# One core: a chunk's sums are split one chunk later, and ScalarE copies products before it splits operands

## The chip, the cores and the metric

The kernel runs on one core of a Trainium2 chip. The metric is the device time of one execution in microseconds. The core has TensorE (PE, matrix products), VectorE (DVE), ScalarE (ACT), GpSimd (POOL) and SyncE (SP, which here only issues DMAs). Each engine works through its own instructions in the order in which they were written; an instruction that waits holds up everything behind it on that engine.

## The reference

The program computes, for 4 batches of 448 rows:

```
attn = sigmoid(q k^T / sqrt(64) - log(448)) v           # 12 heads of 64
h    = relu(x w_in);  u, v = halves of h (512 each)     # x: 768 wide
v_n  = (v - mean) / sqrt(var + 1e-6)
x    = (u * (w_spatial v_n + b_spatial)) w_out          # back to 768
xn   = (x - mean) / sqrt(var + 1e-6) * g_ln
out  = x + relu(xn w_ch1) w_ch2                         # 768 -> 3072 -> 768
```

Everything is float32. Each operand of a product is split into a rounded high part and a remainder, and each product is three matmuls (high x high, high x low, low x high).

## The kernel before, in words

Attention and the first block (hv, hu, spatial) come first and fill some 330 us. Then come the stages that the change touches.

**Projection (class Project, the loop over NCH = 14 chunks of 128 rows).** A chunk is a row block of x. `step(c)` does, on each engine in this order:

- TensorE: 24 matmuls of chunk c, then the six transposes of chunk c - 2 (`turn`, L679).
- ScalarE: copies chunk c out of PSUM (L634); scales the transposes of chunk c - 2 by g_ln (six L681, into a stage); casts their halves to high parts (L299, an instruction for two operands and one for a third); casts the sums of chunk c - 2 (L299).
- VectorE: normalises chunk c - 1 (L649); statistics of chunk c (two L489, one L491); subtracts high parts from the halves (two L300) and from the sums (one L300) of chunk c - 2, which gives the remainders; prepares the scale of chunk c (L482, `rs`).
- GpSimd: four subtractions on the stage of chunk c - 2 (L686 to L689), which give the sums in the one buffer `t`; then the power that makes the scale of chunk c out of `rs` (L483).
- SP: stores the chunk (L635), and from chunk 7 on also the split operands (L670, `out`), since the second half's operands wait in memory.

The halves and sums are the operands of a seven-product scheme (two by two blocks with seven instead of eight products): R11, R21, T2 come from the halves, T1, T3, R22 and T4 from the sums. For chunks 0 to 6 the fourth sum goes into a buffer of its own (`t4`), and `last_sums` splits it for all seven chunks at once. Chunks 7 to 13 put four sums into `t`. A stage has two buffers, `t` has one, the stored operands have one buffer for the first three and two for the sums.

During chunks 9 to 12 the loop also makes the first group's weight sums (`left.sums`, four GpSimd instructions L753 to L756), and splits three of them (`left.put`).

**Groups (function mlp).** Each of 24 rounds (two halves of the rows, 12 groups of 256 hidden units) multiplies in the order L11 R11, L12 R21, S2 T2, S1 T1, S3 T3, L22 T4, S4 R22. L and S are weight operands, R and T row operands. The products share a few PSUM buffers: `pa` takes L11 R11, S2 T2, S3 T3 and L22 T4 one on top of the other, and ScalarE copies it between (`ta`, `tb`, `tc_`, L866, L883, L891); TensorE may add the next product to `pa` only when the copy is done. VectorE adds `pb` and `pd` to those copies; `put` makes the hidden units with a relu (L853) and their remainder (L854).

Round k = 0 also has what the projection left over: the turns of chunks 12 and 13, the normalisation of chunk 13, the splits of the remaining weights, and the next round's weight sums on VectorE. At its end SP loads the two weights of the second half of the round (`w2c`, `w2d`, L726) and the rows for the final sum; `w2c.split` and `w2d.split` (L735 on ScalarE, L736 on GpSimd) stand before the next round's first copy.

Of the kernel before, what the change touches and what calls it, by code (L numbers as in the profile page):

```python
# [18 lines left out]
B, H, S, D = 4, 12, 448, 64  # L19
# [20 lines left out]
HCH = HT // P  # L40
KH = KC // 2
# [182 lines left out]
def sigmoid_attention_gmlp_mlp(ctx: ExitStack, tc, q, k, v, w_in, w_sp, w_out, g_ln, w1, w2, out):  # L224
# [73 lines left out]
    def split(hi, lo, x, eng=nc.vector):  # L298
        nc.scalar.copy(hi, x)  # L299
        eng.tensor_sub(lo, x, hi)  # L300
# [311 lines left out]
    class Project:  # L612
# [4 lines left out]
        def __init__(self, wo, gb, ys_r, xn_r, stage_r, t, t4):  # L617
            self.wo, self.gb, self.ys_r, self.xn_r, self.stage_r = wo, gb, ys_r, xn_r, stage_r
            self.t, self.t4 = t, t4
            self.late, self.turns, self.out_r, self.out_t = None, [], None, None  # L620

        def step(self, c, g):
# [14 lines left out]
            mv = norm_stats([y2[:, 0], y2[:, 1]])  # L637
            if len(self.turns) > 1:
                self.turn()
# [32 lines left out]
        def turn(self):  # L672
# [17 lines left out]
            if c >= HCH:  # L690
                self.out_now = self.out_t.next()
            split(*self.parts(c, 0, 2), x1)
            split(*(a[:, 0] for a in self.parts(c, 2, 1)), x2[:, 1])
            self.out(c, 0, 3)
            n = 3 if c < HCH else 4
            split(*self.parts(c, 3, n), t[:, :n])
# [72 lines left out]
    def mlp(first, proj, after):  # L769
# [58 lines left out]
        for k, (h, g) in enumerate(todo):  # L828
# [33 lines left out]
            pa = ps1()  # L862
            if k == 0:
                left.put("S1", "S3")
            P_(pa, "L11", "R11", True)
            nc.scalar.copy(ta, pa[:, :S])  # L866
# [3 lines left out]
            if k == 0:  # L870
                left.put("L22")
                proj.norm()
# [4 lines left out]
            if k == 0:  # L877
                left.put("S4")
                proj.turn()
                nxt.sums(nc.vector)  # L880
            pre.pop(1)
            P_(pa, "S2", "T2", False)
            nc.scalar.copy(tb, pa[:, :S])  # L883
            pd = ps1()
            P_(pd, "S1", "T1", True)
            pre.pop(2)
# [6 lines left out]
            if k == 0:  # L893
                proj.turn()
                nxt.put("L11", "L12")
            next(chunks, None)
            put(1, 1, tc_)
            if k:
                w2c.load()
                if nxt:  # L900
                    nxt.put("L11")
# [9 lines left out]
            if k == 0:  # L911
                nxt.put("S1", "S3")
# [227 lines left out]
    for c in range(NCH):  # L1140
# [6 lines left out]
        elif c == HCH:  # L1147
            left.load()
        elif c == HCH + 1:
            proj.last_sums()  # L1150
        elif c == HCH + 2:
            left.sums()
            after.load()
        elif c > HCH + 2 and c < HCH + 6:
            left.put(("L11", "L12", "S2")[c - HCH - 3])
# [76 lines left out]
```

## Time and profile before

Three runs took 1114.56, 1116.41 and 1117.33 us, median 1116.41. The profiled execution took 1114.5 us, with a span of 1112.7 us.

| stretch, us | what runs | us | TensorE busy, us | granted clock |
|---|---|---|---|---|
| 331.0 to 360.4 | chunks 3 to 8 | 29.40 | 29.40 | 1.00 |
| 360.4 to 380.6 | chunks 9 to 12 | 20.20 | 19.84 | 1.00 |
| 380.6 to 396.5 | chunk 13, first two products | 15.90 | 11.44 | 0.79 |
| 396.5 to 418.8 | rest of round 0 | 22.30 | 15.22 | 0.77 |
| 418.8 to 427.1 | round 1, first two products | 8.30 | 5.70 | 0.79 |
| 427.1 to 430.4 | round 1, third product | 3.30 | 3.27 | 0.51 |
| 430.4 to 445.0 | round 1, rest | 14.60 | 14.01 | 1.00 |

Times are microseconds from the span's start. Chunks and products are named by what TensorE works on, and it runs ahead of the other engines by one or two chunks. A clock of 1.00 is 2.4 GHz, 0.50 is 1.2 GHz; values between are means over a stretch. A wait is put down to the instruction that released it last. Over the whole span TensorE is busy 96%, VectorE 62%, ScalarE 41%, GpSimd 29%.

### The profile page before, as it was taken

What the parts mean: (1) busy time and instruction counts of PE and PEld (TensorE: products, weight loads), DVE (VectorE), ACT (ScalarE), POOL (GpSimd) and SP (SyncE); (2) the same over time, 40 slices, a digit from 0 to 9 for tenths busy, and PEclk for the clock granted to TensorE, in tenths of its full rate; (3) what the DMA queues carried; (4) which work ended last, traced back from release to release, by engine and by line L of the source; (5) the groups of instructions that cost most, each with busy time, mean ns of one, the idle gap of its engine ahead of it and who ended that gap; (6) DMA issues with size and microseconds to landing.
All of it is one profiled execution on the core that took longest, in us unless ns stands there. A gap on an engine that the chain in (4) does not pass through costs nothing.

```text
span 1112.7 us, 15188 instructions
## 1 busy us (share of the span) xinstructions
PE 1064.4 (96%) x5644; PEld 926.0 (83%) x5644; DVE 690.8 (62%) x1072; ACT 459.4 (41%) x820; POOL 321.3 (29%) x292
## 2 busy tenths in 40 slices
PE   8999999999999878999999999899999999999997
PEld 5466666668899867888888888899999999999997
DVE  4743446447657766888888898853555555555543
ACT  6755556554537654333333333320422222222210
POOL 1231212202207643333222233343322222222210
PEclk9999999999999888999999999999999999999999
DMA  8756869835522557555455455478411111111103
GB/s 239 221 170 203 277 173 337 302 120 183 162 76 101 202 209 269 164 185 164 156 178 183 153 169 171 151 314 275 126 57 57 58 57 57 58 57 57 58 29 100
DMA packets 72730, 174.54 MB, mean 157 GB/s; under 512 B 12560, under 2 KB 31376, under 8 KB 71632
## 3 DMA queue, kind: packets, MB, share of 16 engines
q1 hardware_dynamic: 68368, 151.73, 42.1%
q0 software_dynamic: 3168, 19.73, 5.0%
q10 hardware_dynamic: 1120, 2.11, 0.6%
q8 instruction: 44, 0.72, 0.3%
q14 instruction: 30, 0.25, 0.1%
HBM read 126.67 MB, written 46.87 MB: 156 GB/s over the span
## 4 chain that ended last, share of the span: by engine, by line
PE 67%; DVE 16%; issue 7%; ACT 4%; POOL 3%; DMA 2%; SPq 0%; POOLq 0%; DVEq 0%; ACTq 0%
PE ps L269 19%; PE ps L270 18%; PE ps L271 18%; PE ps L466 6%; PE ps L450 5%; DVE f_mlp L290 3%; DVE r_base L300 2%; DVE r_base L854 2%; DVE f_mlp L289 2%; DVE r_mlp L300 2%; DVE f_base L793 2%; DVE f_mlp L293 2%; ACT r_base L853 1%; ACT f_mlp L681 1%; DVE f_mlp L793 1%
## 5 line engine op out<-in xcount | busy, mean ns | idle before, releaser
L269 PE MATMUL ps<-r_mlp,r_base 128*128 128x384 f32 (+1 forms) x946 | 331.6, 351 | 21.0 <-DVE f_base L793 14.8
L270 PE MATMUL ps<-r_mlp,r_base 128*128 128x384 f32 (+1 forms) x946 | 326.4, 345 | 2.9 <-POOL r_mlp L736 2.9
L271 PE MATMUL ps<-r_mlp,r_base 128*128 128x384 f32 (+1 forms) x946 | 325.9, 345 | 0.0
L736 POOL TENSOR_TENSOR r_mlp<-f_base,r_mlp 128x768 fp32r<-128x768 f32 x48 | 91.8, 1914 | 424.4 <-ACT r_mlp L735 424.4
L269 PEld LDWEIGHTS ps<-r_mlp,r_base 128*128 128x128 f32 x946 | 178.4, 189 | 37.8 <-DVE f_base L793 21.2
L270 PEld LDWEIGHTS ps<-r_mlp,r_base 128*128 128x128 f32 x946 | 178.5, 189 | 7.0 <-POOL r_mlp L736 3.4
L271 PEld LDWEIGHTS ps<-r_mlp,r_base 128*128 128x128 f32 x946 | 178.4, 189 | 2.9
L269 PE MATMUL ps<-r_base 128*128 128x448 f32 (+1 forms) x348 | 132.4, 381 | 1.4 <-ACT r_base L299 1.4
L271 PE MATMUL ps<-r_base 128*128 128x448 f32 (+1 forms) x348 | 130.0, 374 | 0.4 <-DVE r_base L300 0.4
L270 PE MATMUL ps<-r_base 128*128 128x448 f32 (+1 forms) x348 | 130.0, 373 | 0.0
L793 DVE TENSOR_TENSOR f_mlp<-ps,f_mlp 128x768 f32<-128x768 f32 (+1 forms) x97 | 91.7, 945 | 51.5 <-PE ps L271 51.4
L454 ACT ACTIVATE f_att<-ps,bias_s 128x896 f32<-128x896 f32 x96 | 91.5, 1005 | 27.4 <-PE ps L450 27.0
L866 ACT COPY f_base<-ps 128x448 f32<-128x448 f32 x24 | 12.8, 533 | 193.4 <-PE ps L271 193.4
L853 ACT ACTIVATE r_base<-f_base 128x448 fp32r<-128x448 f32 x72 | 41.7, 579 | 107.0 <-DVE f_base L909 46.9
L793 DVE TENSOR_TENSOR f_base<-ps,f_base 128x768 f32<-128x768 f32 x72 | 68.6, 953 | 25.0 <-PE ps L271 24.2
L450 PEld LDWEIGHTS ps<-r_att 64*128 64x128 f32 x576 | 51.0, 189 | 36.6 <-issue 20.4
L450 PE MATMUL ps<-r_att 64*128 64x448 f32 x576 | 75.0, 390 | 5.9 <-ACT f_att L454 4.3
L437 POOL TENSOR_TENSOR r_att<-f_att,r_att 128x512 fp32r<-128x512 f32 x22 | 29.9, 1359 | 174.6 <-DVE r_att L433 160.7
L269 PEld LDWEIGHTS ps<-r_base 128*128 128x128 f32 x348 | 65.5, 188 | 15.6 <-issue 6.5
L466 PE MATMUL ps<-f_att 128*64 128x448 f32 x384 | 77.5, 545 | 0.0
L271 PEld LDWEIGHTS ps<-r_base 128*128 128x128 f32 x348 | 65.6, 189 | 8.7 <-DVE r_base L300 0.8
L270 PEld LDWEIGHTS ps<-r_base 128*128 128x128 f32 x348 | 65.7, 189 | 6.6
(131 smaller groups left out, 1568.0 us busy)
## 6 DMA issues: line engine op xcount, KB each, us to landing
f_base<-wscr SPq DMA_DIRECT2D x95, 384.0 KB, 3.7
f_mlp<-in_w SPq DMA_DIRECT2D x56, 384.0 KB, 3.3
f_att<-in_w SPq DMA_DIRECT2D x20, 768.0 KB, 5.4
wscr<-f_mlp SPq DMA_DIRECT2D x56, 192.0 KB, 1.9
wscr<-f_att SPq DMA_DIRECT2D x20, 384.0 KB, 5.9
f_att<-in_v SPq DMA_DIRECT2D x24, 256.0 KB, 5.0
f_base<-in_w_in SPq DMA_DIRECT2D x8, 768.0 KB, 4.7
f_att<-in_k SPq DMA_DIRECT2D x45, 128.0 KB, 5.2
```

The lines of the kernel that those rows point to most:

```text
L269: nc.tensor.matmul(ps, lh, rh, start=first, stop=False, **more)
L270: nc.tensor.matmul(ps, lh, rl, start=False, stop=False, **more)
L271: nc.tensor.matmul(ps, ll, rh, start=False, stop=last, **more)
L290: nc.vector.scalar_tensor_tensor(bits, low, 29, bits, op0=ALU.logical_shift_right, op1=ALU.bitwise_or)
L300: eng.tensor_sub(lo, x, hi)
L437: eng.tensor_sub(kl, kr, kh)
L450: nc.tensor.matmul(ps[:, j, :S], a[w][rows, kc], a[x][rows], start=(i == 0), stop=(i == 2))
L454: nc.scalar.activation(af, ps[:, :, :S], AF.Sigmoid, bias=bias_s, scale=1.0 / math.sqrt(D))
L466: nc.tensor.matmul(a["ps"][rows, :S], a["v"][:, 4 * j + c], af[:, j], start=(c == 0), stop=(c == 3))
L736: nc.gpsimd.tensor_sub(self.lo, self.blk.ap(WC), self.hi)
L793: nc.vector.tensor_add(y[:, hs], ps, y[:, hs])
L853: nc.scalar.activation(hi, src, AF.Relu)
```

## The change

The sums of a chunk are cast and subtracted in a function of their own, `put_sums`, which `step` calls in the following chunk, after that chunk's statistics and before its own turn. `last_sums` moves from chunk 8 to chunk 9. In round 0 ScalarE's copies of the first two products come before the splits of weights that stood ahead of them, the turns of chunks 12 and 13 come later, and three calls of `put_sums` finish chunks 11 to 13. All other rounds are as before.

```diff
@@ class Project
             self.late, self.turns, self.out_r, self.out_t = None, [], None, None
+            self.summed = None
@@ step
             mv = norm_stats([y2[:, 0], y2[:, 1]])
+            self.put_sums()
             if len(self.turns) > 1:
                 self.turn()
@@ turn
             nc.gpsimd.tensor_sub(t4, x1[:, 1], t[:, 1])
-            if c >= HCH:
-                self.out_now = self.out_t.next()
             split(*self.parts(c, 0, 2), x1)
             split(*(a[:, 0] for a in self.parts(c, 2, 1)), x2[:, 1])
             self.out(c, 0, 3)
+            self.summed = c
+
+        def put_sums(self):
+
+            if self.summed is None:
+                return
+            c, self.summed = self.summed, None
             n = 3 if c < HCH else 4
-            split(*self.parts(c, 3, n), t[:, :n])
+            if c >= HCH:
+                self.out_now = self.out_t.next()
+            split(*self.parts(c, 3, n), self.t.ap(4, KH, D)[:, :n])
             self.out(c, 3, n)
@@ mlp
             pa = ps1()
+            P_(pa, "L11", "R11", True)
+            nc.scalar.copy(ta, pa[:, :S])
             if k == 0:
                 left.put("S1", "S3")
-            P_(pa, "L11", "R11", True)
-            nc.scalar.copy(ta, pa[:, :S])
             if late is not None:
                 late.split()
                 late = None
             if k == 0:
-                left.put("L22")
+                proj.put_sums()
                 proj.norm()
             pb = ps1()
             P_(pb, "L12", "R21", True)
             nc.vector.tensor_add(ta, pb[:, :S], ta)
             put(0, 0, ta)
             if k == 0:
-                left.put("S4")
-                proj.turn()
-                nxt.sums(nc.vector)
+                left.put("L22")
             pre.pop(1)
             P_(pa, "S2", "T2", False)
             nc.scalar.copy(tb, pa[:, :S])
+            if k == 0:
+                left.put("S4")
+                nxt.sums(nc.vector)
             pd = ps1()
             P_(pd, "S1", "T1", True)
+            if k == 0:
+                proj.turn()
             pre.pop(2)
...
             nc.vector.tensor_add(tc_, pd[:, :S], tc_)
             if k == 0:
-                proj.turn()
                 nxt.put("L11", "L12")
             next(chunks, None)
             put(1, 1, tc_)
+            if k == 0:
+                proj.put_sums()
+                proj.turn()
...
             put(0, 1, tb)
             if k == 0:
+                proj.put_sums()
                 nxt.put("S1", "S3")
@@ loop over chunks
-        elif c == HCH + 1:
+        elif c == HCH + 2:
             proj.last_sums()
-        elif c == HCH + 2:
             left.sums()
             after.load()
```

Lines after the first insertion are numbered higher in the changed kernel: L649 is L651 there, L686 to L689 are L688 to L691, L735 is L744, L853 and L854 are L862 and L863, L866 is L873.

VectorE, from one normalisation to the next in the middle of the first half (`r_base` 2x192 and 192 are the halves' remainders, `r_mlp` 3x192 the sums'). Before:

```order
L649 TENSOR_SCALAR f_mlp<-f_base,mv,rs 128x768
L489 BN_STATS st_2800<-f_base 128x6 x2
L491 BN_AGGR mv<-st_2800 128x2
L300 TENSOR_TENSOR r_base<-f_mlp,r_base 128x2x192
L300 TENSOR_TENSOR r_base<-f_mlp,r_base 128x192
L300 TENSOR_TENSOR r_mlp<-f_mlp,r_mlp 128x3x192
L482 TENSOR_SCALAR rs<-mv 128x1
```

and now:

```order
L651 TENSOR_SCALAR f_mlp<-f_base,mv,rs 128x768
L489 BN_STATS st_2798<-f_base 128x6 x2
L491 BN_AGGR mv<-st_2798 128x2
L300 TENSOR_TENSOR r_mlp<-f_mlp,r_mlp 128x3x192
L300 TENSOR_TENSOR r_base<-f_mlp,r_base 128x2x192
L300 TENSOR_TENSOR r_base<-f_mlp,r_base 128x192
L482 TENSOR_SCALAR rs<-mv 128x1
```

The subtraction of the sums stood after the halves and ahead of the scale; it now stands right after the statistics, ahead of the halves, and belongs to the chunk before theirs.

GpSimd, one chunk of the first half, with the semaphores that each instruction waits for. Before:

```order
L686 TENSOR_TENSOR f_mlp<-f_mlp 128x192 [waits Activation_49]
L687 TENSOR_TENSOR f_mlp<-f_mlp 128x192 [waits Activation_49,Pool_49]
L688 TENSOR_TENSOR f_mlp<-f_mlp 128x192 [waits Pool_49]
L689 TENSOR_TENSOR f_mlp<-f_mlp 128x192
L483 TENSOR_TENSOR rs<-rs,mhalf 128x1 [waits DVE_49]
```

and now:

```order
L688 TENSOR_TENSOR f_mlp<-f_mlp 128x192 [waits DVE_49,Activation_49]
L689 TENSOR_TENSOR f_mlp<-f_mlp 128x192 [waits Activation_49,Pool_49]
L690 TENSOR_TENSOR f_mlp<-f_mlp 128x192 [waits Pool_49]
L691 TENSOR_TENSOR f_mlp<-f_mlp 128x192
L483 TENSOR_TENSOR rs<-rs,mhalf 128x1 [waits DVE_49]
```

The order is the same, but the first of the four subtractions now waits for VectorE too: for the subtraction that reads the sums of the chunk before out of `t`.

ScalarE at the end of round 0, from about the casts of chunk 13's operands to the second round's first copy (`r_base` 4x192 is the cast of the sums, `ps` marks products, `r_mlp` 128x768 the weights of the second half). Before:

```order
L299 CAST r_base<-f_mlp 128x4x192
L299 CAST r_base<-f_base 128x384
L299 CAST r_mlp<-f_base 128x384
L853 ACTIVATE r_base<-f_base 128x7x64
L853 ACTIVATE r_base<-ps_3398 128x7x64
L299 CAST r_mlp<-f_base 128x384
L853 ACTIVATE r_base<-f_base 128x7x64
L299 CAST r_mlp<-f_base 128x384 x2
L299 CAST r_base<-f_mlp 128x384
L299 CAST r_base<-f_base 128x384
L735 CAST r_mlp<-f_base 128x768 x2
L866 COPY f_base<-ps_3572 128x448
```

and now:

```order
L299 CAST r_base<-f_mlp 128x192
L862 ACTIVATE r_base<-ps_3395 128x7x64
L299 CAST r_mlp<-f_base 128x384
L862 ACTIVATE r_base<-f_base 128x7x64
L299 CAST r_base<-f_mlp 128x4x192
L299 CAST r_mlp<-f_base 128x384 x2
L299 CAST r_base<-f_mlp 128x384
L299 CAST r_base<-f_base 128x384
L744 CAST r_mlp<-f_base 128x768 x2
L873 COPY f_base<-ps_3572 128x448
```

The cast of the last sums stood right behind the casts of the halves; it now stands behind the relu of the round's last product.

## Rows read from the trace of the kernel before

**Rows 1.** The page's first line

```profile
span 1112.7 us, 15188 instructions
```

**Rows 2.** Waits of TensorE, 315 to 470 us: waiting line, releaser, total us, times, longest

```profile
PE ps L269 <- ACT f_base L866: 5.5, 2, 3.2
...
PE ps L679 <- DVE f_mlp L649: 5.2, 3, 4.5
```

**Rows 3.** One stretch: us, PE, PEld, DVE, ACT, POOL busy us (instructions), clock, DMA share, GB/s

```profile
427.10:430.40 3.30, 3.27 (x9) 2.94 (x10) 2.07 (x2) 0.58 (x1) 2.24 (x2) 0.51 1.04 401
```

**Rows 4.** Timeline of TensorE, three places: start us, length us, line, operation, tiles, [idle before]

```profile
335.88 0.38 PE L679 MATMUL ps<-warm,f_mlp 128*128 128x128 f32 x2
...
360.35 0.38 PE L679 MATMUL ps<-warm,f_mlp 128*128 128x128 f32 x2
...
427.13 0.74 PE L269 MATMUL ps<-r_mlp 128*128 128x448 f32 x1 [2.25 <-ACT f_base L866]
```

**Rows 5.** Timeline of VectorE, 336 to 419 us, columns as in Rows 4

```profile
336.62 0.15 DVE L482 TENSOR_SCALAR rs<-mv 128x1 f32<-128x1 f32 x1
...
337.43 0.68 DVE L649 TENSOR_SCALAR f_mlp<-f_base,mv,rs 128x768 f32<-128x768 f32 x1 [0.67 <-POOL rs L483]
...
339.20 1.18 DVE L300 TENSOR_TENSOR r_base<-f_mlp,r_base 128x384 fp32r<-128x384 f32 x2
...
340.90 0.76 DVE L300 TENSOR_TENSOR r_mlp<-f_mlp,r_mlp 128x576 fp32r<-128x576 f32 x1 [0.52 <-ACT r_mlp L299]
...
382.00 0.96 DVE L300 TENSOR_TENSOR r_base<-f_mlp,r_base 128x768 fp32r<-128x768 f32 x1 [3.27 <-ACT r_base L299]
...
383.94 1.02 DVE L649 TENSOR_SCALAR f_mlp<-f_base,mv,rs 128x768 f32<-128x768 f32 x1 [0.44 <-POOL rs L483]
...
395.76 1.02 DVE L649 TENSOR_SCALAR f_mlp<-f_base,mv,rs 128x768 f32<-128x768 f32 x1 [0.45 <-POOL rs L483]
...
402.66 0.62 DVE L875 TENSOR_TENSOR f_base<-ps,f_base 128x448 f32<-128x448 f32 x1
...
418.34 0.96 DVE L300 TENSOR_TENSOR r_base<-f_mlp,r_base 128x768 fp32r<-128x768 f32 x1 [1.35 <-ACT r_base L299]
```

**Rows 6.** Timeline of GpSimd, 335 to 381 us, columns as in Rows 4

```profile
335.16 0.71 POOL L689 TENSOR_TENSOR f_mlp<-f_mlp 128x192 f32<-128x192 f32 x1
...
336.84 0.55 POOL L483 TENSOR_TENSOR rs<-rs,mhalf 128x1 f32<-128x1 f32 x1 [0.97 <-DVE rs L482]
...
337.74 0.82 POOL L686 TENSOR_TENSOR f_mlp<-f_mlp 128x192 f32<-128x192 f32 x1 [0.35 <-ACT f_mlp L681]
...
340.13 0.72 POOL L689 TENSOR_TENSOR f_mlp<-f_mlp 128x192 f32<-128x192 f32 x1
...
373.45 0.55 POOL L483 TENSOR_TENSOR rs<-rs,mhalf 128x1 f32<-128x1 f32 x1 [2.00 <-DVE rs L482]
...
373.97 1.02 POOL L753 TENSOR_TENSOR f_base<-f_base 128x384 f32<-128x384 f32 x1
...
377.19 1.33 POOL L756 TENSOR_TENSOR f_base<-f_base 128x384 f32<-128x384 f32 x1
...
378.49 0.71 POOL L686 TENSOR_TENSOR f_mlp<-f_mlp 128x192 f32<-128x192 f32 x1
...
380.52 0.59 POOL L689 TENSOR_TENSOR f_mlp<-f_mlp 128x192 f32<-128x192 f32 x1
```

**Rows 7.** Timeline of ScalarE, 404 to 419 us, columns as in Rows 4

```profile
404.19 1.65 ACT L681 ACTIVATE f_mlp<-ps,f_base 128x128 f32<-128x128 f32 x6
...
405.88 0.77 ACT L299 CAST r_base<-f_mlp 128x384 fp32r<-128x384 f32 x2
...
418.21 0.51 ACT L299 CAST r_base<-f_base 128x384 fp32r<-128x384 f32 x1
```

**Rows 8.** Chain that ended last, 413 to 432 us: start us, length us, what

```profile
420.29 5.50 DMA f_base<-wscr
...
425.81 0.83 ACT r_mlp L735
```

## The prediction

> **What bounds the kernel now.** I read the page first, then the stretches, then TensorE's waits, then each engine's timeline through the projection and the first expert group. The page gives a span of 1112.7 us [rows 1]; the profiled run took 1114.5 us, 1.8 us more around the span. TensorE is busy nearly everywhere; the change touches only the fourteen projection chunks and the first group, about 331 to 427 us. From chunk to chunk TensorE keeps a beat of (360.35 - 335.88) / 5 = 4.89 us there [rows 4]. It falls out of step in a few places: 4.5 us for the normalised chunk 10, 3.2 us behind ScalarE's copy of the first product [rows 2], 2.25 us before the second group's third product [rows 4], and after such waits the matmuls run at the lower clock (0.51 granted, from 427.1 to 430.4 us, with TensorE busy throughout) [rows 3]. The change aims at ScalarE, which stands at a cast until GpSimd has finished four subtractions.
>
> The reader should look at one ring in VectorE's and GpSimd's rows. For chunk c: GpSimd's power, VectorE's normalisation, the statistics of the next chunk, the splits of an older chunk, then the scale for the next power. In steady state this ring turns once a chunk and hides under TensorE's beat. GpSimd's four subtractions lie beside it, since they wait only for ScalarE.
>
> **What the change does to that ring.** Nothing is removed or added; every instruction only stands elsewhere. VectorE's subtraction that reads the four sums now comes one chunk later, after the next statistics. The sums have one buffer, t. So GpSimd's first subtraction of a chunk may overwrite t only when VectorE has read the chunk before; the order shows that new wait. Behind the waiting subtraction, in GpSimd's queue, stand three more and then the power of the newest chunk, and VectorE's normalisation waits for that. The ring is now closed through GpSimd. One turn, from rows:
>
> - power to normalisation: 337.43 - 336.84 = 0.59 us [rows 5, 6]
> - normalisation, two statistics and their aggregate, to the next subtraction: 339.20 - 337.43 = 1.77 us [rows 5]
> - subtraction of three sums: 0.76 us; of four: 0.96 us [rows 5]
> - hand-over from VectorE to GpSimd: 336.84 - (336.62 + 0.15) = 0.07 us [rows 5, 6]
> - four GpSimd subtractions: 2.62 us (378.49 to 381.11) with VectorE mostly still, 3.11 us (337.74 to 340.85) with VectorE's 1.18 us pair of subtractions beside them and waits for ScalarE between [rows 5, 6]. In the new order the pair runs beside the first two. I take 2.85, between the ends.
>
> That makes 6.04 us with three sums and 6.24 with four, against TensorE's 4.89. The ring becomes the bound as soon as its lead is used up.
>
> The trace prices the subtractions' contention by the 0.49 us between those two sums. The Trainium skill, page "SBUF — State Buffer", section "Who interferes with whom", says that a VectorE instruction with two SBUF inputs and a GpSimd instruction that reads SBUF take turns, and that the loser blocks for the whole instruction. The trace agrees that they disturb each other, not that the full 1.18 us is lost; what the full loss would give is the last rival below.
>
> **Walking it through.** The power of chunk 2 now follows directly on chunk 0's last subtraction, which ends at 335.87 us [rows 6], so normalisation 2 starts near 336.48, 0.95 earlier than today [rows 5]. Seven turns later normalisation 9 starts at 336.48 + 7 x 6.04 = 378.76. TensorE wants chunk 6 normalised at 360.35 [rows 4]; by the ring it starts at 360.64 and ends 0.68 later, so a wait of about 1.1 us comes there and at each following chunk.
>
> Then the weight sums of the first group stand in GpSimd's queue: 373.97 to 378.52, 4.55 us [rows 6]. They start when power 9 ends, at 378.76 - 0.04 = 378.72, and end at 383.27. Chunk 8's four subtractions (2.62, VectorE's splits are over by then) end at 385.89, and normalisation 10 starts 0.59 later, at 386.48. Today it starts at 383.94 [rows 5]. The gain that the change has here (the power no longer waits 2.00 us for the split of the sums [rows 6]) is therefore smaller than what the ring lost before it. Two turns of 6.24 put normalisation 12 at 398.96, against 395.76 today [rows 5].
>
> From there to the last subtraction of sums today takes 419.30 - 395.76 = 23.54 us [rows 5]. With the new order, from like rows (a 384-column cast holds ScalarE for 0.42, a product's copy or relu half 0.45 to 0.5, six scalings 1.69, the pair of casts 0.77 [rows 7]; an add or relu remainder holds VectorE for 0.6 [rows 5]): chunk 11's sums 1.77 + 0.96 + 2.85 = 5.6; their cast 0.84, subtraction 0.96, normalisation 13 0.6 and the first sum of products 0.6, 8.6; on ScalarE a relu, a weight cast, the second copy, a weight cast, scalings, casts, the third copy and two weight casts, 5.5, 14.1; 0.6 for VectorE's third sum of products; relu, chunk 12's sums, scalings, casts, relu, weight cast, 4.6, 19.3; 1.9 until VectorE has the fourth sum; relu half, last cast, last subtraction 2.3. Together 23.6. Copying the products first does free TensorE earlier inside the group, but the last sums now stand behind the group's last product in ScalarE's and VectorE's order, and the two cancel. The last subtraction ends at 398.96 + 23.6 = 422.56, against 419.30: 3.3 us later.
>
> That instant sets the rest. SP sends the last sums, then loads the two weights of the second half; ScalarE casts them (5.50 us of loading, 0.83 for the second cast [rows 8]) and only then copies the second group's first product, for which TensorE waits until 427.13 [rows 4]. 427.13 - 419.30 = 7.83 us, unchanged. TensorE has by then run through the first group and two products and stands some 9 us there instead of 2.25. Its slow stretch afterwards now costs half of 3.3 us [rows 3]; a longer wait could cost from nothing more to 1.1 us more, and I add 0.3.
>
> Moved one step later, the sums of all chunks of the first half (one cast and one subtraction) lie beside GpSimd's work in that step and cost nothing; without that cover VectorE's part would cost at most some 0.5 us. The stores of the sums keep their places but for one step; nobody waits for them but the weights at the end, priced above.
>
> Sum: 3.3 + 0.3 = 3.6 us. Against the profiled run: 1118.1. That run lay 1.9 us under the median of the runs, 1116.41, so the time to compare is **1120.0 us**, at the edge of the 0.3% (3.35 us) that a measurement can tell.
>
> **Bounds.** The subtractions at 2.62 instead of 2.85 in ten turns (seven, two, one in the tail) take 2.3 us off: +1.0 without the clock, 1117.4. At 3.11 they add 2.6; with 1.1 for the clock and 0.5 for the moved cover, +7.5, 1123.9.
>
> **Rivals.**
> - *The waits cancel* (0 to +2.3, at 1117.4): GpSimd's subtractions run at their short time, and the ring costs only what the removed waits bring. For it: the 2.62 us stand in the trace. Against it: the pair of VectorE subtractions begins at the very moment at which GpSimd's first may start.
> - *Faster*: VectorE reaches the old sums before GpSimd wants the buffer, so that the ring stays under 4.89. Then power 9 and power 10 each lose a wait of 2.00 us ([rows 6] for power 9; power 10 waits alike), chunk 10 is normalised 4.0 us earlier, the tail stays 23.6, and the time is 1116.41 - 4 = 1112.4. It decides wherever the four subtractions and the sums' subtraction take under about 2.5 us together; the rows give 3.4 at least.
> - *Heavier*: the ports are lost for the whole 1.18 us, the four take 3.80, a turn 6.99 or 7.19. By the same walk normalisation 9 starts at 385.4, normalisation 12 at 407.5, the last subtraction ends at 432.0: 12.7 us later, 1129.1. Milder members are a clock that falls in the chunk waits too (half pace over a stretch such as the 3.3 us of [rows 3] adds 1.65 to a chunk, 0.5 more than the ring hides, some 3.5 over seven chunks).
>
> **How the numbers follow.** Forecast 0.50, waits cancel 0.20, faster 0.12, heavier 0.18. Of the forecast's half, 0.30 lies over the 0.3% and 0.20 under. Slower: 0.30 + 0.18 = 0.48; same: 0.20 + 0.20 = 0.40; faster: 0.12. The range that leaves out most of the faster case and the far end of the heavier one is 1114.3 to 1124.5; the forecast's own is 1117.4 to 1123.9.
>
> **What would show it.** Right: GpSimd's first subtraction of a chunk waits for VectorE in nearly every chunk; normalisations about 6 us apart up to chunk 9; TensorE's waits for the normalisation about 1 us each from chunk 6 on; the waits behind the first copies smaller than today's 3.2; a wait of some 9 us before the second group's third product, the last subtraction of sums near 422 us. Wrong: normalisations 4.9 us apart, or the wait at the second group's third product staying near 2 us.

## The result, and the profile after

The changed kernel ran 1120.78 to 1126.32 us in six runs, median 1123.78, against a median of 1117.47 (1114.56 to 1119.13, six runs) of the kernel before: ratio 1.0059, 95% interval 1.0036 to 1.0082. It is slower, by 6.3 us between the medians. The profiled execution took 1124.9 us, 10.4 more than the one before; of these, 5.9 come between the copy of chunk 0 and 451 us, and 4.9 far behind the change. Ahead of that copy, where the two kernels do the same, 0.4 had been given back.

The page's first line has the span, 10.4 us longer than in [rows 1]:

```profile
span 1123.1 us, 15198 instructions
```

TensorE's and GpSimd's waits in the same stretch as [rows 2] (waiting line, releaser, total us, times, longest). L873 is the first copy of a round, L688 GpSimd's first subtraction of a chunk, L681 the transposes:

```profile
PE ps L269 <- ACT f_base L873: 15.0, 2, 10.5
...
POOL f_mlp L688 <- DVE r_mlp L300: 13.3, 5, 2.7
...
PE ps L681 <- DVE f_mlp L651: 7.3, 5, 2.6
```

The waits for that copy grew from 5.5 to 15.0 us, one of them alone 10.49. Those for the normalisation grew from 5.2 to 7.3. GpSimd's wait for VectorE is new. The ring can be read in two engines' rows. First VectorE (start, length, operation, [idle before]): a normalisation, then (behind the statistics, left out here) the old chunk's three sums, the pair of subtractions for the next chunk's halves, and the next normalisation:

```profile
347.82 0.68 DVE L651 TENSOR_SCALAR f_mlp<-f_base,mv,rs 128x768 f32<-128x768 f32 x1 [2.18 <-POOL rs L483]
...
349.59 0.70 DVE L300 TENSOR_TENSOR r_mlp<-f_mlp,r_mlp 128x576 fp32r<-128x576 f32 x1
350.22 1.22 DVE L300 TENSOR_TENSOR r_base<-f_mlp,r_base 128x384 fp32r<-128x384 f32 x2
...
353.68 0.68 DVE L651 TENSOR_SCALAR f_mlp<-f_base,mv,rs 128x768 f32<-128x768 f32 x1 [2.18 <-POOL rs L483]
```

And GpSimd in the same turn: a power, the wait for the sums' subtraction, the first and the last of the four subtractions, the next power:

```profile
347.24 0.55 POOL L483 TENSOR_TENSOR rs<-rs,mhalf 128x1 f32<-128x1 f32 x1
350.44 0.78 POOL L688 TENSOR_TENSOR f_mlp<-f_mlp 128x192 f32<-128x192 f32 x1 [2.65 <-DVE r_mlp L300]
...
352.54 0.60 POOL L691 TENSOR_TENSOR f_mlp<-f_mlp 128x192 f32<-128x192 f32 x1
353.10 0.55 POOL L483 TENSOR_TENSOR rs<-rs,mhalf 128x1 f32<-128x1 f32 x1
```

The subtraction of sums ends at 349.59 + 0.70 = 350.29, GpSimd starts at 350.44, its power ends at 353.65, the normalisation starts at 353.68. A turn takes 5.86 us, where TensorE's beat was 4.89 [rows 4]. From chunk 8 on the same engines' rows show what the ring makes of the end (VectorE: the first half's sums of all chunks, normalisations 9, 10 and 12, the last subtraction of sums):

```profile
375.12 1.89 DVE L300 TENSOR_TENSOR r_base<-f_mlp,r_base 128x1344 fp32r<-128x1344 f32 x1
378.54 1.35 DVE L651 TENSOR_SCALAR f_mlp<-f_base,mv,rs 128x768 f32<-128x768 f32 x1 [1.54 <-POOL rs L483]
...
386.92 0.68 DVE L651 TENSOR_SCALAR f_mlp<-f_base,mv,rs 128x768 f32<-128x768 f32 x1 [1.54 <-POOL rs L483]
...
399.41 0.68 DVE L651 TENSOR_SCALAR f_mlp<-f_base,mv,rs 128x768 f32<-128x768 f32 x1 [1.55 <-POOL rs L483]
...
423.16 0.96 DVE L300 TENSOR_TENSOR r_base<-f_mlp,r_base 128x768 fp32r<-128x768 f32 x1
```

GpSimd's third subtraction of chunk 7, beside the 1344-column one, and the first weight sum:

```profile
375.67 1.79 POOL L690 TENSOR_TENSOR f_mlp<-f_mlp 128x192 f32<-128x192 f32 x1
...
378.48 0.99 POOL L762 TENSOR_TENSOR f_base<-f_base 128x384 f32<-128x384 f32 x1
```

That subtraction took 1.79 us instead of 0.60, which made the turn to normalisation 9 7.03 us long. The last subtraction ends at 424.12, 4.82 us later than in [rows 5]. From there the chain that ended last runs as before (start, length, what; [rows 8]):

```profile
423.16 0.97 DVE r_base L300
...
424.60 0.46 SPq L735
...
425.11 5.51 DMA f_base<-wscr
...
430.64 0.83 ACT r_mlp L744
431.47 0.44 ACT f_base L873
...
431.96 0.74 PE ps L269
```

The store, then the load of 5.51 us, the cast, the copy, and TensorE's third product of round 1 at 431.96, against 427.13 [rows 4]: 4.83 later. TensorE's stretches around it, with the columns of [rows 3]:

```profile
427.10:431.96 4.86, 0.00 (x1) 0.00 (x1) 0.58 (x2) 2.09 (x3) 1.40 (x1) 0.50 1.01 370
431.96:436.80 4.84, 4.84 (x13) 4.32 (x14) 2.03 (x2) 1.11 (x2) 2.19 (x2) 0.50 1.03 400
```

It stands idle and then works 4.84 us at 0.50 of the clock (1.2 GHz); before, 3.3 us at 0.51 [rows 3]. That adds 0.7. TensorE's next wait, behind the first addition of the second layer, ends at 450.88 instead of 445.36 us: a difference of 5.5. But the two profiles do not reach the projection at the same time. ScalarE's copy of chunk 0, ahead of everything that the change moves, before and after:

```profile
322.71 0.80 ACT L634 COPY f_base<-ps 128x768 f32<-128x768 f32 x1 [3.01 <-PE ps L271]
...
322.29 0.80 ACT L635 COPY f_base<-ps 128x768 f32<-128x768 f32 x1 [3.02 <-PE ps L271]
```

Counted from that copy, normalisation 12 comes 4.07 us later (3.65 + 0.42), the way from there to the last subtraction is 1.17 longer, and the clock takes 0.7: together 5.9. The 1.17 show in VectorE's rows: the last of round 1's weight sums before, the same one after, and the third sum of products of round 0, for which the rest of the chain waits:

```profile
411.42 0.55 DVE L756 TENSOR_TENSOR f_base<-f_base 128x384 f32<-128x384 f32 x1
...
412.79 0.95 DVE L765 TENSOR_TENSOR f_base<-f_base 128x384 f32<-128x384 f32 x1
...
414.80 0.61 DVE L904 TENSOR_TENSOR f_base<-ps,f_base 128x448 f32<-128x448 f32 x1
```

The last 4.9 of the profiled pair's 10.4 lie between there and 800 us, in rounds that the change leaves as they were. VectorE's rows of two such rounds (its pairs of 384-column subtractions), then GpSimd's subtraction of a weight and TensorE's wait, each for both rounds:

```profile
512.38 0.55 DVE L300 TENSOR_TENSOR r_mlp<-f_base,r_mlp 128x384 fp32r<-128x384 f32 x1
512.85 0.55 DVE L300 TENSOR_TENSOR r_base<-f_base,r_base 128x384 fp32r<-128x384 f32 x1
...
542.34 2.65 DVE L300 TENSOR_TENSOR r_mlp<-f_base,r_mlp 128x384 fp32r<-128x384 f32 x2
```

```profile
512.86 2.21 POOL L745 TENSOR_TENSOR r_mlp<-f_base,r_mlp 128x768 fp32r<-128x768 f32 x1 [10.26 <-ACT r_mlp L744]
...
542.76 1.82 POOL L745 TENSOR_TENSOR r_mlp<-f_base,r_mlp 128x768 fp32r<-128x768 f32 x1 [9.53 <-ACT r_mlp L744]
```

```profile
514.33 0.45 PE L269 MATMUL ps<-r_mlp,r_base 128*128 128x384 f32 x1 [0.88 <-DVE f_base L802]
...
545.91 0.66 PE L269 MATMUL ps<-r_mlp,r_base 128*128 128x384 f32 x1 [2.51 <-DVE f_base L802]
```

Where VectorE's second subtraction starts first (512.85 against 512.86), GpSimd takes 2.21 us and TensorE waits 0.88. Where GpSimd starts first (542.76, VectorE's second being due 0.47 behind 542.34), VectorE's pair takes 2.65 us and TensorE waits 2.51. A round of the second kind, called dear below, is about 0.9 us longer (30.97 against 30.03 from round to round). The profile of before has one of them in ten rounds, that after has five, and behind one of these the clock fell for another 1.6 us. The last of the ten rounds is dear in the profiles of all fourteen kernels of this document; there GpSimd starts even before VectorE's first subtraction (728.34 against 728.38 in the changed kernel). Of the other nine, four are dear in the changed kernel's profile, none in that of before, and none to two in those of the experiments (one with the delay alone, which has the whole loss). Which kind a round becomes hangs on some hundredths of a microsecond, so this part is chance of one execution more than an effect of the change: the medians differ by 6.3, not by 10.4.

### The profile page after: what moved, and what is told of

It is laid out like the page before. It is cut to its first block, busy times and chain, and to the rows that moved or that the text cites. A ratio compares the mean times of both kernels' runs of the same rounds, so it can differ in the third digit from the quotient of the medians.

```text
span 1123.1 us, 15198 instructions
## 1 busy us (share of the span) xinstructions
PE 1060.4 (94%) x5644; PEld 924.5 (82%) x5644; DVE 695.2 (62%) x1072; ACT 458.4 (41%) x820; POOL 315.8 (28%) x292
## 4 chain that ended last, share of the span: by engine, by line
PE 63%; DVE 17%; issue 7%; POOL 4%; DMA 4%; ACT 3%; SPq 1%; POOLq 0%; DVEq 0%; ACTq 0%
PE ps L269 18%; PE ps L270 17%; PE ps L271 17%; PE ps L466 6%; PE ps L450 5%; DVE r_base L300 2%; DVE f_mlp L290 2%; DVE r_mlp L300 2%; DVE r_base L863 2%; DVE f_base L802 2%; DVE f_mlp L289 1%; DVE f_mlp L293 1%; ACT r_base L862 1%; DMA sscr<-vraws 1%; DVE st L489 1%
## 5 line engine op out<-in xcount | busy, mean ns | idle before, releaser
L873 ACT COPY f_base<-ps 128x448 f32<-128x448 f32 x24 | 12.8, 532 | 198.3 <-PE ps L271 198.3
L802 DVE TENSOR_TENSOR f_base<-ps,f_base 128x768 f32<-128x768 f32 x72 | 68.6, 953 | 26.0 <-PE ps L271 25.1
L862 ACT ACTIVATE r_base<-f_base 128x448 fp32r<-128x448 f32 x72 | 41.7, 579 | 104.9 <-DVE f_base L923 46.2
L269 PEld LDWEIGHTS ps<-r_base 128*128 128x128 f32 x348 | 65.3, 188 | 14.2 <-issue 6.5
L300 DVE TENSOR_TENSOR r_base<-f_base,r_base 128x384 fp32r<-128x384 f32 (+1 forms) x105 | 72.8, 713 | 3.2 <-DMA oscr<-r_base 3.2
L271 PEld LDWEIGHTS ps<-r_base 128*128 128x128 f32 x348 | 65.3, 188 | 7.8
```

What stands on the lines that cost most here:

```text
L269: nc.tensor.matmul(ps, lh, rh, start=first, stop=False, **more)
L271: nc.tensor.matmul(ps, ll, rh, start=False, stop=last, **more)
L802: nc.vector.tensor_add(y[:, hs], ps, y[:, hs])
L862: nc.scalar.activation(hi, src, AF.Relu)
```

## The experiments

Every kernel was compared with the kernel before in its own set of runs; that kernel's median was 1117.5 in the first set and 1115.1 to 1115.6 in the others, so ratios are compared, not medians (the times expected in numbers 1 to 4 were written when only the first set was known). "Third product" is TensorE's first product of round 1 that waits for the copy. Times of place are of one profile each. "Chunk 0" is where ScalarE's copy of chunk 0 starts in it, ahead of anything in which these kernels differ: it lies up to 1.6 us apart, so places of two rows are compared from there.

| kernel | chunk 0 | normalisation 12 | last sums end | third product | between | ratio (95%) |
|---|---|---|---|---|---|---|
| before | 322.71 | 395.76 | 419.30 | 427.13 | 7.83 | 1 |
| changed | 322.29 | 399.41 | 424.12 | 431.96 | 7.84 | 1.0059 (1.0036 to 1.0082) |
| round order only | 322.98 | 395.94 | 418.57 | 426.41 | 7.84 | 1.0010 (0.9999 to 1.0022) |
| delay only | 322.92 | 400.06 | 425.20 | 433.05 | 7.85 | 1.0060 (1.0041 to 1.0078) |
| two buffers | 323.83 | 393.96 | 417.65 | 425.50 | 7.85 | 0.9982 (0.9970 to 0.9994) |
| split first | 323.25 | 393.09 | 416.25 | 424.07 | 7.82 | 0.9972 (0.9961 to 0.9983) |
| first half's sums back | 322.34 | 400.64 | 425.42 | 433.26 | 7.84 | 1.0072 (1.0055 to 1.0088) |
| changed, early loads | 322.28 | 399.40 | 424.12 | 426.73 | 2.61 | 1.0020 (1.0006 to 1.0033) |
| before, early loads | 322.28 | 395.24 | 418.77 | 425.97 | 7.20 | 0.9986 (0.9973 to 0.9999) |
| split first, early loads | 322.95 | 393.49 | 416.64 | 419.25 | 2.61 | 0.9948 (0.9930 to 0.9966) |

**1. Only the order of round 0.** The changed kernel, with the sums split in their own turn:

```
             self.summed = c
+            self.put_sums()
 ...
-        elif c == HCH + 2:
+        elif c == HCH + 1:
             proj.last_sums()
+        elif c == HCH + 2:
             left.sums()
```

> The changed kernel with the sums split in the same turn again, and the sums of the first half in the step where they stood; only the first round keeps its new order. Ring theory (the one-chunk delay is what costs): normalisation 12 returns to near 395.8 us, the last subtraction of sums ends at 419 to 420.5 us, TensorE's wait before the second group's third product shrinks from 10.5 to 6 or 7 us, and the time is 1116.5 to 1119. Rival (the order of the first round is what costs): normalisation 12 near 395.8 as well, but the last subtraction still ends at 423 to 424 us, and the time is 1121 to 1124.

Normalisation 12 is back at 395.94, the ratio includes 1. The loss is not in the order of round 0. That order brings nothing by itself either: TensorE gets through round 0 sooner and then waits 7.68 us for the same chain.

**2. Only the delay.** The changed kernel, with round 0 as before and `put_sums` right behind each of its turns:

```
 pa = ps1()
+if k == 0: proj.put_sums()     # chunk 11, then left.put("S1", "S3")
 ...
 proj.turn()
+proj.put_sums()                # at both turns
```

> The changed kernel with the first round in the order of the kernel before (each pair of splits directly behind its turn); only the projection keeps the one-chunk delay. Ring theory: normalisations 5.9 us apart up to chunk 8, normalisation 12 near 399.4 us as in the changed kernel, the last subtraction of sums 23.5 us later at 422.5 to 423.5 us, time 1120.5 to 1123. Rival (the first round's order is what costs): the time falls back to 1116.5 to 1118.5.

Normalisations 5.86 us apart, normalisation 12 at 400.06, and the whole loss (1.0060). The last subtraction came some 2 us later than expected: 0.6 of that is the later start of this profile, and from normalisation 12 to its end took 25.1 us, not 23.5.

**3. Two buffers for the sums.** Nothing moves; odd chunks use other, idle memory:

```
-            t = self.t.ap(4, KH, D)
+            t = self.t_of(c)        # even chunks: as before; odd: a second block
```

> The changed kernel with two buffers for the four sums, so that GpSimd's first subtraction of a chunk no longer waits for VectorE's reading of the chunk before; no instruction moves. Ring theory: that wait is gone, normalisations come 4.9 to 5.2 us apart up to chunk 8, normalisation 12 near 391.5 to 394 us, the last subtraction of sums 24.7 us later at 416.5 to 419 us, time 1113.5 to 1117.5. Rival (the engines' contention for memory stretches the subtractions, the buffer is no matter): normalisations stay 5.5 us or more apart, and the time stays at 1121 to 1124.

Normalisations are 4.9 to 5.7 us apart up to chunk 8 instead of 5.9, normalisation 12 comes 5.45 us earlier than in the changed kernel (7.0 counted from chunk 0), and the time falls below that of the kernel before. The single buffer closes the ring.

**4. The late split ahead of the normalisation.** One buffer, two lines exchanged:

```
+            self.put_sums()
             self.norm()
             mv = norm_stats([y2[:, 0], y2[:, 1]])
-            self.put_sums()
```

> The changed kernel with the late split placed ahead of the step's normalisation instead of behind its statistics: one buffer as before, but VectorE reads the old sums without having to normalise first. Ring theory: the ring through power and normalisation is open, normalisations 4.9 to 5.2 us apart, normalisation 12 near 391.5 to 394.5 us, time 1113.5 to 1117.5, like that with two buffers within 1.5 us. Rivals: by contention alone 1121 to 1124; if any one-chunk wait between GpSimd and VectorE suffices (a second ring, GpSimd's four subtractions, ScalarE's cast, VectorE's subtraction) the normalisations lie 5.3 to 5.8 us apart and the time is 1118 to 1121.

VectorE's rows of one turn (old sums, normalisation, next normalisation), and GpSimd's first subtraction in it:

```profile
347.81 0.76 DVE L300 TENSOR_TENSOR r_mlp<-f_mlp,r_mlp 128x576 fp32r<-128x576 f32 x1 [1.21 <-ACT r_mlp L299]
348.49 0.68 DVE L651 TENSOR_SCALAR f_mlp<-f_base,mv,rs 128x768 f32<-128x768 f32 x1
...
353.38 0.67 DVE L651 TENSOR_SCALAR f_mlp<-f_base,mv,rs 128x768 f32<-128x768 f32 x1
```

```profile
348.72 0.90 POOL L688 TENSOR_TENSOR f_mlp<-f_mlp 128x192 f32<-128x192 f32 x1 [1.21 <-DVE r_mlp L300]
```

GpSimd still waits for VectorE, 1.21 instead of 2.65 us, but VectorE's subtraction no longer waits for a power that stands behind GpSimd's: a turn takes 4.89 us, TensorE's beat. The ratio is that of two buffers. So a wait between the two engines is not what costs, only a wait that comes round to itself and takes longer than the beat.

**5. The first half's sums back in their step.**

```
-        elif c == HCH + 2:
+        elif c == HCH + 1:
             proj.last_sums()
+        elif c == HCH + 2:
             left.sums()
```

> The changed kernel with only the sums of the first half (VectorE's 1344-column subtraction, 1.89 us) back in the step where they stood. If that subtraction is what stretched GpSimd's third subtraction of chunk 7 from 0.60 to 1.79 us, and with it the ninth normalisation's turn from 5.9 to 7.03 us: the turn is 5.9 to 6.1 again, every later normalisation comes 0.9 to 1.2 us earlier, the last subtraction of sums ends at 422.9 to 423.3 us, time 1121.5 to 1123. If it lay beside other work for nothing, as predicted: last subtraction at 424.1, time 1122.5 to 1124.5 as in the changed kernel; a third way, that it stretches something as much where it stood before, gives the same numbers but a longer turn one chunk earlier.

A miss, nearest to the third way. VectorE's rows of normalisation 7, the first half's sums, normalisations 8 and 9:

```profile
365.74 0.68 DVE L651 TENSOR_SCALAR f_mlp<-f_base,mv,rs 128x768 f32<-128x768 f32 x1 [2.86 <-POOL rs L483]
...
372.44 1.56 DVE L300 TENSOR_TENSOR r_base<-f_mlp,r_base 128x1344 fp32r<-128x1344 f32 x1 [3.02 <-ACT r_base L299]
373.91 0.68 DVE L651 TENSOR_SCALAR f_mlp<-f_base,mv,rs 128x768 f32<-128x768 f32 x1
...
379.74 1.37 DVE L651 TENSOR_SCALAR f_mlp<-f_base,mv,rs 128x768 f32<-128x768 f32 x1 [2.16 <-POOL rs L483]
```

The turn to normalisation 9 is 5.83 us again instead of 7.03: the 1344-column subtraction did cost 1.2 there. But with the delay chunk 6's fourth sum is only just ready one step earlier; VectorE stands 3.02 us for the cast of all sums, with the normalisation behind it, and the turn to normalisation 8 grows from 5.85 to 8.17. The move belongs to the delay, and undoing it makes the two turns 1.1 us longer.

**6. Early loads in the changed kernel.** SP loads the weights ahead of the last stores:

```
                 left.put("S4")
+                w2c.load()
+                w2d.load()
                 nxt.sums(nc.vector)
 ...
                 nxt.put("S1", "S3")
-                w2c.load()
-                w2d.load()
```

> The changed kernel, with SyncE told to load the first group's two second-layer weights as soon as their buffers are free, ahead of the last chunks' stores of sums instead of behind them. Theory (the last subtraction of sums sets the end only by way of the store and load queued behind it): the last subtraction stays at 424.1 us, but ScalarE no longer waits 4.87 us for the load; four casts, two weight casts and the copy follow the last sums' cast directly, and the second group's third product starts at 426.9 us instead of 431.96, TensorE's wait there falls from 10.5 to about 5.4 us; time 1117.5 to 1119.5, some 5 us under the changed kernel. Rival (the wait has another cause, ScalarE's or VectorE's own work): third product after 430 us, time 1122 to 1124.5.

ScalarE's casts and copy now follow without a wait, and TensorE's third product comes where expected (its wait 5.27 instead of 10.49). Not all of it is kept: at the first addition of the second layer TensorE then waits 2.67 us instead of 0.94, and goes on at 447.07 instead of 450.88, so 3.8 of the 5.2 us are left.

```profile
424.69 1.56 ACT L744 CAST r_mlp<-f_base 128x768 fp32r<-128x768 f32 x2
426.16 0.52 ACT L873 COPY f_base<-ps 128x448 f32<-128x448 f32 x1
```

```profile
426.73 0.74 PE L269 MATMUL ps<-r_mlp 128*128 128x448 f32 x1 [5.27 <-ACT f_base L873]
```

**7. Early loads in the kernel before** (the same edit):

> The same early loads in the kernel before. Theory: its wait of 2.25 us before the second group's third product disappears, since the casts and the copy would be over near 422 us and TensorE arrives at 424.9; the slow stretch behind it (1.6 us) may go with it: 1111.5 to 1113.5. Rival (the last sums are not what the wait hangs on here): 1115 to 1117.

The median, 1113.37, lies in the expected range, but the ratio makes the gain 1.6 us (0.1 to 3.0), where that range stood for 2.1 to 4.1 under 1115.6. The way was not the expected one either: the third product comes only 1.2 us earlier (0.7 counted from chunk 0), and the wait is 3.20, since TensorE arrives sooner (422.8 instead of 424.9). The casts could not be over at 422 us: in ScalarE's order they stand behind the round's last relu, which waits for VectorE until 421.81.

**8. Split first and early loads.**

> Early loads together with the late split ahead of the normalisation. If the two are independent: last subtraction of sums at 416.3 us as with the split alone, third product of the second group at 419 us instead of 424.07, wait about 5 us, time 1106 to 1108. If they overlap (the wait then stands at something else): 1109 to 1112.

Independent by the places: the last subtraction ends at 416.64 and the third product starts at 419.25, with a wait of 5.26. The median, 1108.04, lies at the upper edge of that range; the ratio is 0.9948 (0.9930 to 0.9966), where the product of the two single ones (0.9972, and 1.0020 / 1.0059) is 0.9933.

**9. Then also the first copy of round 1 ahead of its splits.**

```
 nc.scalar.copy(ta, pa[:, :S])
+if k == 1:
+    left.put("S1", "S3", "L22", "S4")
+    for w in held: w.split()    # w2c, w2d of round 0
 ...
-nxt.put("S1", "S3") ... nxt.put("L22", "S4"); w2c.split(); w2d.split()
```

The load of the third group's weights (`nxt.load`), which stood at the start of round 1, goes behind these splits too.

> The kernel with both, and ScalarE's copy of the second group's first product ahead of the four casts of that group and of its two weight casts (the change's own idea, one group later). Theory: the copy follows the last sums' cast at 415.3 us, the third product starts at 415.8 to 416.5 us, TensorE's wait there is 2 to 2.5 us, time 1103.5 to 1105.5. Rival (the casts put off hold up the fourth product or the second layer): the third product is early, but a new wait of 2 us or more stands before the products S1 or S3, time 1105.5 to 1108.

The place is the rival's: the third product waits 2.15 us, but the fifth one 4.13. TensorE's rows, then VectorE's ahead of the second:

```profile
413.82 0.47 PE L269 MATMUL ps<-r_mlp 128*128 128x448 f32 x1 [2.15 <-ACT f_base L873]
...
421.86 0.47 PE L269 MATMUL ps<-r_mlp 128*128 128x448 f32 x1 [4.13 <-ACT f_base L896]
```

```profile
418.98 1.26 DVE L300 TENSOR_TENSOR r_base<-f_base,r_base 128x384 fp32r<-128x384 f32 x1 [3.24 <-DMA oscr<-r_base]
420.16 0.61 DVE L890 TENSOR_TENSOR f_base<-ps,f_base 128x448 f32<-128x448 f32 x1
```

VectorE's addition, for which ScalarE's relu, behind it the second copy (L896) and then TensorE wait, stands behind a split that may overwrite stored sums only when SP's stores have left (3.24 us). So the cause is this wait, not casts put off. Median 1109.67, above both ranges; ratio 0.9946 (0.9927 to 0.9965), no gain over the last.

**10. The addition ahead of that split.** `left.put("L22", "S4")`, the two weight splits and with them `nxt.load` move behind `put(0, 0, ta)` of round 1.

> The kernel with the early split, the early loads and the early copy, and now also VectorE's addition of the second group's second product ahead of that group's L22 and S4 splits, which stood 3.24 us at the last stores of sums. Theory: the wait of 4.13 us before the group's fifth product shrinks to below 1 us, the rest stays: 3 to 4 us off, median 1104 to 1106.5. Rival (TensorE then waits for L22 or S4 themselves, which no longer lie ahead): a wait of 2 us or more before the products L22 or S4, median 1106.5 to 1109.

```profile
418.59 0.47 PE L269 MATMUL ps<-r_mlp 128*128 128x448 f32 x1 [1.44 <-ACT f_base L898]
...
436.65 0.69 PE L269 MATMUL ps<-r_mlp,r_base 128*128 128x384 f32 x1 [5.66 <-DVE f_base L802]
```

4.13 became 1.44, but a wait of 5.66 stands before the second layer, where there was 2.41. ScalarE there waits 4.44 us for the next group's weights: their cast starts at 426.96, hardly earlier than in number 9 (427.53), while TensorE gets there sooner. The median, 1107.11, misses the 1104 to 1106.5. Ratio 0.9930 (0.9916 to 0.9943), the lowest of all, though its interval overlaps those of numbers 8 and 9.

**11. GpSimd's weight subtraction in halves**, in the changed kernel:

```
-            nc.gpsimd.tensor_sub(self.lo, self.blk.ap(WC), self.hi)
+            for i in range(2): ...      # 384 columns each
```

> The changed kernel with GpSimd's subtraction of each second-layer weight (768 columns, 1.8 us) as two of 384 columns. Theory (a VectorE subtraction that comes while one of GpSimd's runs stands until that one is over): VectorE's pair that took 2.65 us takes at most 1.9, TensorE's waits of 2.5 us in five of ten groups fall to 1.7 or less, the waits for the second layer's additions from 21.9 to 15 to 18 us together, median 1120.5 to 1123. Rival (VectorE loses to both halves, one after the other): waits of 2.5 us stay, 1123 to 1125.

The pair that took 2.65 us is the one ahead of the second layer's additions. In nine of the ten rounds it takes 1.02 us here, as in the changed kernel's cheap rounds. Only in the last round does GpSimd get ahead of it, and there the pair takes 2.65 us still (2.67 beside the whole instruction in the changed kernel), and TensorE waits 2.50:

```profile
722.45 2.27 POOL L747 TENSOR_TENSOR r_mlp<-f_base,r_mlp 128x384 fp32r<-128x384 f32 x2 [9.74 <-ACT r_mlp L744]
...
722.49 2.65 DVE L300 TENSOR_TENSOR r_mlp<-f_base,r_mlp 128x384 fp32r<-128x384 f32 x2
```

So the one encounter went as in the rival: VectorE lost to both halves, one after the other. That one round of ten is dear and not five says nothing for the halves: eight of the profiles with whole instructions have just one as well. In time it is unclear: 1.0051 (1.0036 to 1.0066) against 1.0059 (1.0036 to 1.0082).

**12. All together**: number 10 with the weight splits back behind S1 and S3, and the halves.

> All findings together: the late split ahead of the normalisation, early weight loads, the second group's first copy and second addition ahead of the splits that wait for the stores, its two weight casts right behind S1 and S3, and GpSimd's weight subtractions in halves. Against the best version so far (ratio to the kernel before 0.993) the loads of the third group's weights should go out 1 to 1.5 us earlier, since GpSimd's subtractions free a buffer sooner, TensorE's wait of 5.66 us before the second group's second layer falls to 4 to 4.7, and the groups with waits of 2.5 us behind VectorE become rarer: ratio 0.989 to 0.992. Rival (the wait hangs on another transfer, or the halves cost as much as they free): ratio 0.992 to 0.995.

The rival. ScalarE's cast of the next group's weight, and GpSimd's four halves beside VectorE's splits:

```profile
429.48 0.51 ACT L299 CAST r_base<-f_base 128x384 fp32r<-128x384 f32 x1 [5.21 <-DMA f_base<-wscr]
```

```profile
416.65 4.62 POOL L747 TENSOR_TENSOR r_mlp<-f_base,r_mlp 128x384 fp32r<-128x384 f32 x4 [4.48 <-ACT r_mlp L744]
```

Four halves took 4.62 us, where the two whole ones take 3.94 in number 10 (3.59 in the changed kernel); the load went out no earlier, TensorE's wait is 6.31. Ratio 0.9940 (0.9922 to 0.9959), not distinguishable from number 10.

## Why the prediction was right, and where its sizes were off

- *The ring closes through GpSimd and becomes the bound*: right, and shown by numbers 2 to 4. Turns of 5.86 with three sums and 6.25 with four were measured, 6.04 and 6.24 predicted; the four subtractions took 2.66 to 2.70 us with three sums, near the lower bound of 2.62, and 2.88 with four, where 2.85 was taken for both.
- *Normalisation 12 at 398.96*: it came at 399.41, or 399.83 with chunk 0 where it was before, 0.9 late; errors of both signs met. The six turns without other work gave back 0.7. The sums of the first half, "beside GpSimd's work in that step and cost nothing" (at most 0.5 without cover), stretched GpSimd's subtraction by 1.2, and their turn took 7.03 instead of 6.04. Chunk 8's turn took 8.38 instead of 7.72: the weight sums ran 4.94 us instead of 4.55, and VectorE's splits, "over by then", ran on until 384.5 beside chunk 8's four subtractions (2.99 instead of 2.62).
- *From normalisation 12 to the last subtraction 23.6, "the two cancel"*: this term was mis-sized. It took 24.71, against 23.54 before. The order of round 0 alone makes it 22.6 (number 1), the delay alone 25.1 (number 2): the delay costs more there than the copies win. The 1.2 us lie in one step of the walk. Up to ScalarE's two weight casts it holds (14.25 us, 14.1 predicted), but the "0.6 for VectorE's third sum of products" took 1.75 (the rows of L765 and L904 above). Before that sum VectorE makes four weight sums and the remainders of chunk 12's halves. The four weight sums took 0.55 us each in the kernel before; now the last three take 0.84 to 0.95, beside GpSimd's subtractions of chunk 12 (410.92 to 414.19), which the new order puts at the same time. With two buffers and with the split first, round 0 has the same order, but GpSimd starts these subtractions only as the weight sums end: the sums take 0.55 us each again, and the way takes 23.7 and 23.2 us. These two differ from the changed kernel in more than this, so the overlap as the cause is read from the rows and has no run of its own.
- *7.83 us from there to the third product, unchanged*: 7.82 to 7.85 in the seven profiles of the first seven rows of the table. That this is the store, the load and the casts was shown by number 6, which cuts it to 2.61.
- *Clock +0.3*: it was 0.7, within the bound.
- *Sum 3.6*: by places 4.07 + 1.17 + 0.7 = 5.9, between the forecast's 3.6 and its upper bound of 7.5; measured 6.3 between the medians. The mechanism was right, the size in part luck: the ring as it turned, with the rest as forecast, would have cost some 2.4 us, and the first half's sums (1.2), chunk 8's turn (0.7), the tail (1.2) and the clock (0.4 more) stand where the sum put nothing or too little. The median, 1123.78, lies 0.1 us under the upper end of the forecast's own range, which was set on a base of 1116.41; with six runs that base is 1117.47.
- *What would show it*: GpSimd's wait and the ring's spacing came as said. TensorE's waits for the normalisation were 0.27, 1.04, 0.79, 2.62 and 2.62 us rather than 1 each. The wait behind the first copy of round 0 was to shrink below 3.2; it was 4.55, since ScalarE reaches that copy later. The big wait was 10.49 instead of some 9.
- *Rivals*: "the waits cancel" had the subtractions' time nearly right (2.62), but not the time: its +2.3 at most is a ratio of 1.0021, under the interval. "Heavier" took VectorE's pair to block GpSimd for all of 1.18 us. In the ring GpSimd's first subtraction took 0.78 instead of 0.60, and VectorE's pair 1.22, where it takes 0.82 when GpSimd comes late (at 361.93). The later rounds show the rule of the Trainium skill, page "SBUF — State Buffer", section "Who interferes with whom", at full size: whoever comes second stands for the whole instruction of the other, and 1.82 us of GpSimd's moved VectorE's pair from 1.02 to 2.65. So the rule holds for one instruction, and the rival's price, which took two for one, was too high. "Faster" needed a turn under 4.89; number 4 makes one of just that, and its ratio of 0.9972 puts it at 1113.3 on the prediction's base of 1116.41, where this rival gave 1112.4.

## What to carry to other kernels

Before work is put off by a step, follow the buffer that it reads: with a single buffer the writer inherits the delay, and whatever is queued behind the writer does too. If that chain leads back to the work put off, its turn has to stay under the beat of the engine that sets the pace; a second buffer, or reading the old data first in the step, opens it. And a load queued behind the last stores can make the end of a chain later: here by 5.2 us in the changed kernel, by 0.7 in the kernel before, where other work ends nearly as late.

## What the runs showed of the hardware

- Which of two overlapping subtractions on VectorE and GpSimd stands still was decided by hundredths of a microsecond, and cost TensorE 0.88 or 2.51 us of waiting; the fourteen profiles have one to five dear rounds in ten. That the count also varies between executions of one kernel, and with it their spread of 4 to 6 us, is not shown, since each kernel has one profile.
- A single-input instruction suffers too: a normalisation of 0.68 us took 1.35 beside a GpSimd addition (378.54 above, with the addition from 378.48), and 1.36 in the kernel before (374.04, with the addition from 373.97 [rows 6]).
- After 10.49 us of waiting TensorE ran at 1.2 GHz for the next 4.8 us of work, after 2.51 us in one round for 3.4, and after four other waits of 2.5 not at all. The wait alone does not settle it: after 10.48 us (number 5) and 10.45 us (number 11) the mean clock over the next 4.84 us was 0.58 and 0.64, not 0.50.
